# Chunked attention with a mixture of experts on one core: weight loads from iteration 19 on, a reordered prologue, deeper output buffers, and the conditional in front of slot 22

## The chip, the core and the metric

The kernel runs on one core of one Trainium2 chip. The metric is device time in microseconds (us). PE is the matrix engine, PEld its weight loads, DVE, ACT and POOL are the vector, scalar and general engines, SP issues most DMAs. POOL issues DMAs too, those that cast or scatter; they are called software DMAs below, because the profile lists them under `software_dynamic`.

## What is computed

```python
# attention, per batch b and head h, in 24 chunks of 32 queries
k_full = concat([mem_k, k[l_start:r_end]])     # 8 memory rows, then 16 + 32 + 8 rows of context
a = softmax(q_c @ k_full.T / 8)
x[token] = a @ concat([mem_v, v[l_start:r_end]])        # 3072 tokens, 8 heads x 64 = 512
# then a dense part and a mixture of 8 experts, one expert a token
y_dense = relu(x @ w1_dense) @ w2_dense
logits = x @ w_gate;  e = argmax(logits)
y_moe = softmax(logits)[e] * (relu(x @ w1[e]) @ w2[e])
out = y_dense + y_moe
```

## The kernel before, in words

The order of the instructions on every engine is the order of the program: the schedule is written by hand. A tile is 128 tokens, and there are 24 of them.

**Prologue** (lines 522 to 550). POOL issues the loads of k and q, a pair of heads each (`load_qk`). SP issues the memory rows of V (`load_mem_rows`, 8 small DMAs), the first V tile (`load_v(0)`), the gate's weights and `load_v(1)`. DVE clears `kbds[0]` and `mkbd`, the block-diagonal keys of the first batch and of the memory. `transposes(0)` gives eight steps, k and q by turns for four head pairs: PE transposes, ACT copies q; of k ACT copies the half of the first head (L352) and DVE that of the second (L350). After each second step DVE clears a quarter of `kbds[1]` (L545). Then `mem_keys` turns the memory keys.

**Attention loop** (L600). Iteration i holds stages of several tiles: the scores of tile i, turning and values of the tiles before, the gate and the dense part of older ones. On DVE an iteration has one `mx` (L385). `qk_at` gives the k and q loads of an iteration, and at odd i `load_v((i + 5) // 2)` issues ten or more DMAs on SP. `shift(i)` copies V rows within and between V tiles (L294, L297), so it needs the next V tile. In iteration 0 POOL and DVE make constants; in iteration 3 POOL asks for the first half of the dense weights; in iteration 4 come the table constants (L165 to L182). In the iterations of `W_AT`, 16 to 21, `next_w` asks for one half of an expert's weights each. The list starts with both halves of expert 0, the second dense half, then both halves of expert 1, of 2 and so on, 17 in all. Finished rows of x go to the DRAM buffer `xs` with `scatter` (L515), an indirect DMA on POOL, sorted by expert.

**End of the loop** (L652 to L685). The last stages are written out; one `next_w` stands in their middle.

**Slots** (`run`, L854). A slot is 128 rows of one expert. 28 slots always run, and 14 more stand in two nested conditionals (L899, L901) behind them; on these inputs they are not taken. In slot n: `between(n)` may ask for weights (`W_SLOT`), `bring` finds the weights of the next slot, `first` is the first matmul (L802), `second` the dense and the expert's second one (L818, L821), `turn` transposes the rows of the next slot, `send` scales, adds and issues the output (L847, an indirect DMA on POOL). The rows of a slot come with `fetch`, a DMA on SP, six slots ahead. `send` writes `gw`, `to` and `o`, which have three buffers each; `to` and `o` are free again when their output has landed. Slots 0 to 2 are of experts 0, 1 and 2.

The value that decides the conditional (`nov`, computed on DVE in the first slots) is read by every engine with `values_load` at L897, after the last slot.

Of the kernel before, what the change touches and what calls it, by code (L numbers as in the profile page):

```python
# [48 lines left out]
W_AT = (16, 17, 18, 19, 20, 21)  # L49
W_SLOT = (1, 2, 4, 6, 7, 9, 10, 12, 13, 15)  # L50
SOON = 9
NXG = 6
EARLY = 3
# [5 lines left out]
def kernel(  # L59
# [149 lines left out]
    with ExitStack() as one:  # L209
# [152 lines left out]
        def attention(g, qT, kbd):  # L362
# [4 lines left out]
            def scores():  # L367
                sc = ps.tile([128, H, KEYS], F32, tag="ps", name="sc")
                for hp in range(HP):
                    nc.tensor.matmul(sc[:, 2 * hp:2 * hp + 2, CTX:],  # L370
                                     qT[:, hp, 128 * t:128 * t + 128],
                                     mkbd[:, b * HP + hp], start=True, stop=True)
                for hp in range(HP):
                    for cc in range(4):
                        n0 = 128 * t + 32 * cc
                        nc.tensor.matmul(sc[32 * cc:32 * cc + 32, 2 * hp:2 * hp + 2, :CTX],  # L376
                                         qT[:, hp, n0:n0 + 32],
                                         kbd[:, hp, :, n0:n0 + CTX],
                                         start=True, stop=True, tile_position=(0, 32 * cc))
# [5 lines left out]
                nc.vector.reduce_max(mx, sc, axis=AX.X)  # L385
# [145 lines left out]
        for _ in range(2 * (HP - 1)):  # L531
            load_qk()
        load_mem_rows(0, B)
        load_v(0)
        nc.vector.memset(kbds[0], 0.0)  # L535
        nc.vector.memset(mkbd, 0.0)
        load_mk()
        make_identity(nc, identf)
        nc.sync.dma_start(wgate, moe_w_gate.rearrange("(t p) m -> p t m", p=128))
        load_v(1)  # L540
        turned, steps = transposes(0)
        for n, step in enumerate(steps):
            step()
            if n % 2:
                nc.vector.memset(kbds[1][:, n // 2], 0.0)  # L545
        mem_keys()
# [53 lines left out]
        for i in range(NT):  # L600
# [84 lines left out]
        scatter(n)  # L685

# [14 lines left out]
    with ExitStack() as two:  # L701
# [61 lines left out]

        first_x = w2.tile([128, 1], F32, name="first_x", bufs=1)

        def fetch(j):
            xg = w3.tile([128, ROW], F32, tag="xg", name="xg", bufs=NXG)
# [6 lines left out]
        def turn(j):  # L774
# [4 lines left out]
            xT = w3.tile([128, DT + FT, 128], BF16, tag="xT", name="xT", bufs=2)  # L779
# [4 lines left out]
        def bring(j):  # L784
# [7 lines left out]
            wa = w2.tile([128, DT, 512], BF16, tag="wa", name="wa")  # L792
# [40 lines left out]
        def send(j):  # L833
            xg = xgs.pop(j)
            gw = w3.tile([128, 1], F32, tag="gw", name="gw")
            nc.vector.reciprocal(gw, xg[:, ROW - 2:ROW - 1])  # L836
            to = w3.tile([128, 1], I32, tag="to", name="to")
# [6 lines left out]
            o = w3.tile([128, DM], F32, tag="o", name="o")  # L844
# [38 lines left out]
        for j in js[EARLY:EARLY + NXG - 1]:  # L883
            fetch(j)
        def between(n):
# [3 lines left out]
            if n in W_SLOT:  # L889
                next_w()  # L890

# [5 lines left out]
        count = nc.values_load(nov[:1, :1], min_val=0, max_val=NOVER)  # L897

        with tc.If(count > SURE - SLOW, preferred_fallthrough_block=False):  # L899
# [33 lines left out]
```

## Time and profile before

| | |
|---|---|
| median of 3 runs | 268.08 us (266.94 to 270.17) |
| the profiled execution | 266.79 us |
| its span, first to last instruction | 265.1 us |
| PE busy | 214.4 us (81%) |
| DVE, ACT, POOL busy | 167.6, 148.8, 146.9 us |
| mean granted PE clock | 0.947 |
| software DMAs | 28.38 MB, 55.4% of the DMA engines' span |
| DMAs issued by SP | 17.46 MB, 29.0% |
| HBM | 45.26 MB read, 15.76 MB written |

A row of the timeline reads: start, duration, engine, line, operation, out<-in, shapes, count, and in brackets the idle time of the engine before it and what ended it. A q behind an engine's name is its sequencer, which waits, branches and issues. "issue" stands for idle time that nothing in the profile explains. A row of the waits reads: who waited, for whom, us in total, how often, the longest.

### The profile page before, as it was taken

To read this page: it belongs to the slowest core of one execution; us is meant where nothing else is said; L and a number is where in the kernel's file an instruction comes from. 1 tells how busy PE (TensorE), PEld (TensorE's weight loads), DVE (VectorE), ACT (ScalarE), POOL (GpSimd) and SP (SyncE) were. 2 spreads that over 40 slices of the span, in tenths; PEclk is the share of its full clock that TensorE was granted. 3 is DMA by queue.
4 is the path that set the end of the run, shared out by engine and by line. 5 is a ranking of instruction groups with operands and counts; after the bars stand their busy time and mean duration, and the time that the engine had idled before them with its cause. 6 is when DMAs were issued, how large, how long until landed. Compare 5 with 4: busy or idle time off the path is not lost. (4 is left out here: it accounts for less than half of the span.)

```text
span 265.1 us, 9702 instructions
## 1 busy us (share of the span) xinstructions
PE 214.4 (81%) x3808; PEld 161.6 (61%) x3843; DVE 167.6 (63%) x421; ACT 148.8 (56%) x279; POOL 146.9 (55%) x228
## 2 busy tenths in 40 slices
PE   1545889998999985973997797999899998999930
PEld 1324677787787874752785674667566665666710
DVE  7566866889889996844598623884454343556520
ACT  2534766976896776470476463556455555455520
POOL 8748334697777985653376654344545352333420
PEclk9999967999999999796599999999999999999995
DMA  6999975799989999999773195599999999551120
GB/s 87 184 198 180 186 127 100 130 176 222 205 205 193 227 230 161 195 163 233 124 123 122 42 190 223 163 239 294 260 271 203 270 285 259 174 161 53 48 109 2
DMA packets 56833, 46.50 MB, mean 175 GB/s; under 512 B 30158, under 2 KB 49102, under 8 KB 56784
## 3 DMA queue, kind: packets, MB, share of 16 engines
q0 software_dynamic: 22656, 28.38, 55.4%
q1 hardware_dynamic: 34128, 17.46, 29.0%
q8 instruction: 32, 0.52, 0.8%
q14 instruction: 17, 0.14, 0.2%
HBM read 45.26 MB, written 15.76 MB: 230 GB/s over the span
## 5 line engine op out<-in xcount | busy, mean ns | idle before, releaser
L847 POOL DMA_INDIRECT out_dram<-o,to x28 | 31.1, 1109 | 52.1 <-DVE o L845 42.4
L781 ACT COPY xT<-xt 128x512 bf16<-128x512 bf16 x28 | 16.4, 585 | 39.6 <-DVE gw L836 35.5
L845 DVE TENSOR_TENSOR o<-py,oe 128x512 f32<-128x512 f32 x28 | 19.3, 690 | 20.7 <-ACT oe L843 19.2
L515 POOL DMA_INDIRECT xs<-row,si x24 | 26.4, 1099 | 9.3 <-issue 4.0
L440 POOL CAST xT<-x 128x512 bf16<-128x512 f32 x22 | 13.6, 616 | 31.0 <-ACT x L437 28.2
L821 PE MATMUL py<-wall,h 128*128 128x512 bf16 (+1 forms) x111 | 28.7, 379 | 1.0 <-DMA wall<-in_moe_w_dram 1.0
L448 PEld LDWEIGHTS pg<-wgate,x 128*128 128x128 f32 x192 | 26.5, 202 | 4.5 <-ACT x L437 1.0
L409 PE MATMUL xp<-vw,aT 64*32 64x65 f32 x1280 | 20.4, 240 | 9.3 <-DVE vw L297 6.1
L392 ACT ACTIVATE a<-a 128x512 f32<-128x512 f32 x24 | 15.1, 630 | 22.6 <-DVE a L387 21.4
L455 PE MATMUL ph<-wall,xT 128*128 128x512 bf16 x75 | 23.6, 403 | 4.4 <-ACT a L392 1.8
L352 ACT COPY kbd<-tp 64x768 bf16<-64x768 bf16 x28 | 22.1, 790 | 7.9 <-DVE kbd L535 4.2
L818 PE MATMUL py<-wall,xT 128*128 128x512 bf16 x99 | 25.9, 379 | 0.8
L428 POOL CAST row<-xn 128x512 bf16<-128x512 f32 x24 | 21.3, 886 | 8.7 <-DVE xn L421 8.5
L448 PE MATMUL pg<-wgate,x 128*128 128x8 f32 x192 | 24.6, 255 | 0.1
L409 PEld LDWEIGHTS xp<-vw,aT 64*32 64x32 f32 x1280 | 15.9, 113 | 13.9 <-issue 7.1
L294 DVE COPY vw<-vw 24x1820 f32<-24x1820 f32 x17 | 21.1, 1240 | 0.7 <-DMA vw<-in_v_dram 0.2
L385 DVE TENSOR_REDUCE mx<-sc 128x8 f32<-128x512 f32 x24 | 16.6, 690 | 7.1 <-PE sc L376 6.5
L843 ACT ACTIVATE oe<-py,gw 128x512 f32<-128x512 f32 x28 | 19.4, 692 | 2.1 <-PE py L821 2.1
L397 PE MATMUL ap<-identf,a 128*128 128x128 f32 x96 | 17.1, 306 | 4.2 <-ACT a L392 4.0
L802 PEld LDWEIGHTS <-wall 128*128 128x128 bf16 x256 | 15.6, 98 | 5.3 <-issue 2.0
L437 ACT COPY x<-xtp 128x512 f32<-128x512 f32 x24 | 14.1, 586 | 7.5 <-PE xtp L435 6.6
L421 DVE TENSOR_TENSOR xn<-xp,rs 128x512 f32<-128x512 f32 x24 | 16.6, 692 | 2.3
(162 smaller groups left out, 464.8 us busy)
## 6 DMA issues: line engine op xcount, KB each, us to landing
wall<-in_moe_w_dram POOLq DMA_DIRECT2D x16, 512.0 KB, 9.4
xg<-xs SPq DMA_DIRECT2D x25, 257.0 KB
kb<-in_k_dram POOLq DMA_DIRECT2D x16, 192.0 KB, 6.5
qb<-in_q_dram POOLq DMA_DIRECT2D x16, 192.0 KB, 6.7
vw<-in_v_dram SPq DMA_DIRECT2D x48, 64.0 KB
xs<-wall SPq DMA_DIRECT2D x8, 257.0 KB
vw<-in_v_dram SPq DMA_DIRECT2D x32, 56.0 KB
vw<-mtpl SPq DMA_DIRECT2D x20, 65.0 KB
```

Of the source, the lines that this page charges most:

```text
L294: eng(vw[r + 32:r + 56, :PC - 1], vw[r:r + 24, 1:])
L352: nc.scalar.copy(dst, tv[r])
L409: nc.tensor.matmul(xp[32 * cc:32 * cc + 32, par, (D + 1) * hp:(D + 1) * (hp + 1)], st["aT"][r, hp, 32 * cc:32 * cc + 32], vw[r, 4 * (g % 2 ...
L428: nc.gpsimd.tensor_copy(row[:, :XW].bitcast(BF16), st["xn"])
L448: nc.tensor.matmul(grp["pg"][:, u, :], st["x32"][:, d, :], wgate[:, d, :], start=(d == 0), stop=(d == DT - 1))
L455: nc.tensor.matmul(ph, st["xT"][:, d, :], wall[:, E, d, :], start=(d == 0), stop=(d == DT - 1))
L515: i = nc.gpsimd.indirect_dma_start(xs[:, :], bass.IndirectOffsetOnAxis(ap=grp["si"][:, u:u + 1], axis=0), row.bitcast(I32), None, bounds_c ...
L818: nc.tensor.matmul(py, xts[j][:, DT + f, :], wall[:, E, DT + f, :], start=(f == 0), stop=(f == FT - 1))
L821: nc.tensor.matmul(py, hs[j][:, f, :], w[:, f, :], start=(f == 0), stop=(f == FT - 1))
L843: nc.scalar.activation(oe, hs[j, False], AF.Copy, scale=gw)
L845: nc.vector.tensor_tensor(o, hs[j, True], oe, ALU.add)
L847: i = nc.gpsimd.indirect_dma_start(out[:, :], bass.IndirectOffsetOnAxis(ap=to, axis=0), o, None, bounds_check=NT * 128 - 1, oob_is_err=False)
```

## The change

Four parts of the program change.

1. Weights. `W_AT` becomes 19 to 23, five in place of six; a second `next_w` stands behind the last `scatter`. The first half of the dense weights is asked for in iteration 4 in place of 3.
2. Prologue. POOL loads k and q of two head pairs, then the memory keys, then the other two pairs. `load_v(0)`, the gate's weights and `load_v(1)` come after the fourth transposing step, and so does `mem_keys`. `kbds[0]` is cleared in quarters, each in front of its steps; the last quarter of `kbds[1]` is cleared in iteration 0, and the table constants are made there too. The scores' two loops over head pairs become one.
3. Buffers. `gw` and `o` have six buffers, `to` has eight.
4. Conditional. The value is read, and the 14 conditional slots stand, in front of slot 22 in place of behind slot 27. Their `xg`, `xT` and `wa` have tiles of their own (the tag's added "m").

```diff
-W_AT = (16, 17, 18, 19, 20, 21)
+W_AT = (19, 20, 21, 22, 23)
+REST = 22
...
                     nc.tensor.matmul(sc[:, 2 * hp:2 * hp + 2, CTX:], ...
-                for hp in range(HP):
                     for cc in range(4):
...
-        for _ in range(2 * (HP - 1)):
+        for _ in range(2):
             load_qk()
         load_mem_rows(0, B)
-        load_v(0)
-        nc.vector.memset(kbds[0], 0.0)
+        load_mk()
+        for _ in range(4):
+            load_qk()
+        make_identity(nc, identf)
         nc.vector.memset(mkbd, 0.0)
-        load_mk()
-        make_identity(nc, identf)
-        nc.sync.dma_start(wgate, moe_w_gate.rearrange("(t p) m -> p t m", p=128))
-        load_v(1)
         turned, steps = transposes(0)
         for n, step in enumerate(steps):
+            if n % 2 == 0:
+                nc.vector.memset(kbds[0][:, n // 2], 0.0)
             step()
-            if n % 2:
+            if n == 3:
+                mem_keys()
+                load_v(0)
+                nc.sync.dma_start(wgate, moe_w_gate.rearrange("(t p) m -> p t m", p=128))
+                load_v(1)
+            if n % 2 and n < 2 * HP - 1:
                 nc.vector.memset(kbds[1][:, n // 2], 0.0)
-        mem_keys()
...
             if i == 0:
+                nc.vector.memset(kbds[1][:, HP - 1], 0.0)
                 constants()
-            if i == 3:
+                table_constants()
+            if i == 4:
                 load_w(E, 0)
-            if i == 4:
-                table_constants()
...
         scatter(n)
+        next_w()
...
-            gw = w3.tile([128, 1], F32, tag="gw", name="gw")
+            gw = w3.tile([128, 1], F32, tag="gw", name="gw", bufs=6)
...
-            to = w3.tile([128, 1], I32, tag="to", name="to")
+            to = w3.tile([128, 1], I32, tag="to", name="to", bufs=8)
...
-            o = w3.tile([128, DM], F32, tag="o", name="o")
+            o = w3.tile([128, DM], F32, tag="o", name="o", bufs=6)
...
+        def rest():
+            own[0] = "m"
+            with tc.If(count[0] > SURE - SLOW, preferred_fallthrough_block=False):
+                start(more[:2])
+                with tc.If(count[0] > SURE - SLOW + 2, preferred_fallthrough_block=False):
+                    start(more[2:])
+            own[0] = ""
...
             if n in W_SLOT:
                 next_w()
+            if n == REST:
+                count.append(nc.values_load(nov[:1, :1], min_val=0, max_val=NOVER))
+                rest()
...
-        count = nc.values_load(nov[:1, :1], min_val=0, max_val=NOVER)
-        with tc.If(count > SURE - SLOW, preferred_fallthrough_block=False):
-            start(more[:2])
-            with tc.If(count > SURE - SLOW + 2, preferred_fallthrough_block=False):
-                start(more[2:])
```

More of the change, by code (lines that the diff above doesn't have):

```diff
@@ L762, in table @@
                                         op0=ALU.is_gt, op1=ALU.mult)]
+        own = [""]
         first_x = w2.tile([128, 1], F32, name="first_x", bufs=1)
         def fetch(j):
-            xg = w3.tile([128, ROW], F32, tag="xg", name="xg", bufs=NXG)
+            xg = w3.tile([128, ROW], F32, tag="xg" + own[0], name="xg", bufs=NXG)
             read_rows(xg, rowi[:, j:j + 1])
@@ L791, in bring @@
             ev = nc.vector.value_load(expi[:1, k:k + 1], min_val=0, max_val=n - 1)
-            wa = w2.tile([128, DT, 512], BF16, tag="wa", name="wa")
+            wa = w2.tile([128, DT, 512], BF16, tag="wa" + own[0], name="wa")
             nc.vector.tensor_copy(
@@ L884 @@
             fetch(j)
+        def rest():
[5 more added lines that the diff above has]
+            own[0] = ""
+        count = []
         def between(n):
```

2 lines of the change are left out of this document (1 added, 1 removed).

## The prediction

> **What bounds the kernel now.** I read the page first (span, clock and DMA slices), then the windows around the throttled stretches, then the timeline of the stages that the edits touch.
>
> ```profile
> span 265.1 us, 9702 instructions
> DMA  6999975799989999999773195599999999551120
> 107.40:110.90 3.50, 3.28 (x56) 2.23 (x50) 3.05 (x5) 1.97 (x4) 2.96 (x3) 0.51 1.10 219
> 121.10:131.30 10.20, 7.46 (x130) 5.89 (x132) 5.41 (x10) 2.09 (x4) 2.01 (x3) 0.50 0.96 184
> 163.40:253.20 89.80, 85.40 (x870) 58.53 (x884) 48.21 (x148) 48.20 (x83) 38.67 (x39) 1.00 0.81 206
> ```
> In the window rows the columns are stretch, length, busy time of PE, PEld, DVE, ACT and POOL, granted clock, DMA share, GB/s. From 163.4 on (the expert slots) PE is busy 85.4 of 89.8 us: a stall of PE there is lost time. Before that the DMA engines are full (9s) up to about 125 us, and twice the clock is halved.
>
> ```profile
> 94.65 0.68 DVE L385 TENSOR_REDUCE mx<-sc 128x8 f32<-128x512 f32 x1
> 97.14 0.85 POOL L91 DMA_DIRECT2D wall<-in_moe_w_dram  x1
> 106.08 0.38 PE L376 MATMUL sc<-kbd,qT 128*32 128x112 bf16 x16 [2.88 <-issue]
> 110.02 6.25 SPq L275 DMA_DIRECT2D vw<-in_v_dram  x8
> 122.98 0.29 DVE L297 COPY vw<-vw 24x260 f32<-24x260 f32 x1 [2.61 <-DMA vw<-in_v_dram]
> 123.62 1.40 PE L409 MATMUL xp<-vw,aT 64*32 64x65 f32 x58 [6.12 <-DVE vw L297]
> 135.27 0.68 DVE L385 TENSOR_REDUCE mx<-sc 128x8 f32<-128x512 f32 x1
> 139.33 0.69 DVE L385 TENSOR_REDUCE mx<-sc 128x8 f32<-128x512 f32 x1
> 145.17 0.69 DVE L385 TENSOR_REDUCE mx<-sc 128x8 f32<-128x512 f32 x1
> ```
> L385 starts once an iteration; these rows are iterations 15, 21, 22 and 23. The first weight goes out at 97.14, in iteration 16. SP issues the V loads one behind the other, eight in 6.25 us from 110.02. PE stands 2.88 us with no releaser shown and 6.12 us for V rows of iteration 19, and each stall brings a halved clock.
>
> **The change part by part** (minus is time gained).
>
> Weights from iteration 19 on. Iterations 16 to 23 take 145.17 - 94.65 = 50.5 us. Undisturbed, I put iteration 16 at 4.3 us, 17 at 5.0 (transposes), 18 to 20 at 4.3, 21 at 4.9 (it chooses experts), 22 at 4.06 (139.33 - 135.27), and 23 at 5.84 as it was (145.17 - 139.33): 37.0. The 4.3 and 4.9 are estimates just above the 4.06 row. Three weights leave the stretch in which the last V loads run, so these land before iterations 18 to 21 ask for them. But five weights now run beside iterations 19 to 23, so I add 1.6 us, half of such a stall as 2.88 us: 38.6, a gain of **-11.9**. Ends: -13.5 with no stall; -4.3 with two stalls of 2.88, each with a halved 3.4 us window (1.7 us).
>
> The dense weights one iteration later (3 to 4):
> ```profile
> 33.31 0.71 POOL L236 DMA_DIRECT2D qb<-in_q_dram  x1
> 41.64 0.61 PE L455 MATMUL ph<-wall,xT 128*128 128x512 bf16 x1
> DMA to landing us min/median/max: 8.2/9.9/10.7
> ```
> The issue would follow the q load of 33.31, some 7.6 us ahead of its first use at 41.64, against 8.2 to 10.7 us of landing: up to 3 us of wait. Against it, the early V loads have the DMA engines to themselves for one iteration longer. I take **0**, ends -3 and +3.
>
> The prologue:
> ```profile
> 6.50 0.79 ACT L352 COPY kbd<-tp 64x768 bf16<-64x768 bf16 x1 [4.17 <-DVE kbd L535]
> 7.33 0.96 DVE L350 COPY kbd<-tp 64x768 bf16<-64x768 bf16 x1 [0.78 <-ACT kbd L352]
> 8.52 0.72 DVE L545 MEMSET kbd<- 128x792 uint32 x1 [0.23 <-issue]
> 2.71 0.27 DVE L266 MEMSET ve<- 32x256 f32 x1
> 15.46 0.85 PE L339 MATMUL tp<-ident,qb 128*64 128x128 bf16 x12 [0.47 <-DMA qb<-in_q_dram]
> 15.87 0.96 DVE L350 COPY kbd<-tp 64x768 bf16<-64x768 bf16 x1 [0.96 <-ACT kbd L352]
> 17.77 0.46 DVE L327 COPY mkbd<-mkt 64x128 bf16<-64x128 bf16 x2
> 18.32 0.17 DVE L142 MEMSET ones<- 128x128 bf16 x1
> 19.42 0.69 DVE L385 TENSOR_REDUCE mx<-sc 128x8 f32<-128x512 f32 x1
> 35.40 0.17 DVE L173 CAST thr<-thr_i 128x22 f32<-128x22 int32 x1
> 36.82 0.15 DVE L182 MEMSET low<- 128x1 f32 x8
> ```
> Before, PE waits for k and q from DMA (0.47 us at the last one). V(0) and its loads on SP now stand behind the fourth transpose, so k and q land earlier, though the two memory-key loads pass four of them on POOL's queue. But the clearing of kbds[0], one memset before, becomes four, each on DVE in front of its pair of copies, and DVE's copy waits for ACT's (7.33 follows 6.50 + 0.79). So for each head pair now follow one another: clear 0.72, ACT copy 0.79, DVE copy 0.96, gap 0.23, clear of kbds[1] 0.72, some 0.13 between them: 3.55 us, more than DMA needs. From the first DVE copy at 6.96 (ACT no longer waits the 0.4 us for the long memset) three such rounds, the copy 0.96 and what step 3 puts in between (L327 0.46, four memsets of 0.27, gaps 0.1) end the last copy at 20.2, against 15.87 + 0.96 = 16.8. Behind it on DVE, ahead of the first mx, stand 0.23 + 0.72 for the last clear, 0.17 for ones, POOL's select and first iota (an estimate: 0.6 with the hand-overs), the table constants (35.40 to 36.97, 1.6 us), and 0.3: mx at 23.9 instead of 19.42, **+4.5**. All PE work waits for it. What leaves iteration 4 was beside PE work there: 0 back. V(0), wgate and V(1) queue on SP behind memsets that end at about 13; V(0) is first read in iteration 1, so this hides. Ends: -2.4 (the copies hide and k and q set the pace, 15.46 becoming 13), +6.
>
> Experts' slots:
> ```profile
> 163.94 0.97 POOL L515 DMA_INDIRECT xs<-row,si  x1 [0.30 <-issue]
> 171.71 1.03 PE L821 MATMUL py<-wall,h 128*128 128x512 bf16 x4
> 188.24 1.05 PE L802 MATMUL ph<-xT,wa 128*128 128x128 bf16 x16
> 192.69 1.05 PE L802 MATMUL ph<-xT,wa 128*128 128x128 bf16 x16 [1.23 <-DVE xT L780]
> DVE to L839 <- DMA out_dram<-o,to: 12.2, 11, 2.9
> 224.87 1.02 PE L821 MATMUL py<-wall,h 128*128 128x512 bf16 x4 [0.95 <-DMA wall<-in_moe_w_dram]
> ```
> The last weight of expert 2 now goes out after the last scatter (163.94 + 0.97 = 164.9) and slot 2 wants it at 171.71, 6.8 us later, with landings of 8.2 to 10.7 measured in a fuller DMA: **+1.2**, ends 0 and +3.2. It also stands on POOL ahead of the first reads' marker and runs beside these reads.
>
> Deeper buffers: DVE waits 12.2 us for old output rows before it can write `to`; of this PE feels what a slot lasts beyond its PE work, 85.40 / 28 = 3.05 us by the window row: 1.4 us at the quoted slot (192.69 - 188.24 = 4.45). For the other ten waits together I estimate 1.2 us, since most are shorter than DVE's slack: -2.6. Faster slots meet the same weights, and the wait of 0.95 at 224.87 grows by about 1: **-1.6**, ends -3.1 and +0.5.
>
> The conditional in front of slot 22, and the end:
> ```profile
> L899 PEldq COMPARE_BRANCH  x2: 93/2070/4047, 254.0 to 254.6; - x2
> L899 ACTq COMPARE_BRANCH  x2: 38/44/49, 254.8 to 255.1; - x2
> L899 POOLq INC_SWDGE_SEM  x1: 1147/1147/1147, 258.9 to 258.9; - x1
> L928 POOLq DRAIN  x3: 51/103/3992, 260.3 to 264.8; - x3
> 253.21 1.02 PE L821 MATMUL py<-wall,h 128*128 x4
> 255.96 0.97 POOL L847 DMA_INDIRECT out_dram<-o,to  x1 [1.46 <-DVEq L899]
> ```
> PE's second branch, over the slots not taken, lasts 4.05 us, from 254.6 to 258.65, 4.4 us after the last matmul (253.21 + 1.02). At the end this hides behind POOL; in front of slot 22 six slots of PE work queue behind it. With its restart 4.7 us. Such a stop halves the clock: stops of 2.88 and 6.12 us left halved stretches of 3.4 and 10.2 us, the latter with 7.7 us after PE had resumed at 123.62; between them I take 5.2 us at half speed, 2.6 us. Together **+7.3**. ACT's branches take 0.05 us and DVE's work has slack. On POOL all output rows must land and 1.15 us follows, with slot 22's output behind it; PE's own stop covers that. Ends: +1.0 (branch as short as ACT's, the loads remain), +8.6.
>
> [...]
>
> At the end the last output starts at 255.96 and the span ends 9.1 us later: landing at about 258.9 (INC_SWDGE_SEM waits for it), 1.15, POOL's 3.99 us drain, 0.8. Without the conditional the drain can start once the output is issued: 1.0 + 4.0 + 0.8 = 5.8, **-3.3**. Ends -1.2 (only INC_SWDGE_SEM goes) and -4.6 (the drain shrinks). The merged loop of the scores only orders 20 matmuls anew: 0; the extra tags take SBUF alone: 0.
>
> Sum: -11.9 + 0 + 4.5 + 1.2 - 1.6 + 7.3 - 3.3 = -3.8. The profiled execution took 266.79, so 263.0; the median of the runs is 1.29 above it, so 264.3.
>
> **The rivals.** (a) The prologue gets faster: DVE's copies need not follow ACT's, and k and q set the pace. Against it stand four waits on ACT in the rows of that kind. Term -2.0 instead of +4.5: 257.8. (b) PE's branch costs what ACT's does, the target being loaded already: term +1.0: 258.0. Against it: 4.05 us over the same untaken slots. [...] (c) The slower side: weights at 19 to 23 stall PE twice as at 106.08, since DMA is still full of V loads there. Term -4.3: 271.9. All other terms add to +8.1, so the kernel is slower from the point at which this gain falls under 8.1. For it speaks that the DMA slices read 9 to about 125 us; against it that the last V loads move earlier.
>
> **How the numbers follow.** The sum 0.46 (own range 260 to 268.5), (a) 0.15, (b) 0.15, (c) 0.20, others 0.04. The range 257.5 to 272 reaches from the two fast rivals to the slow one. A measurement tells about 1% from no change: 265.4 and 270.8 are the bounds. Of the sum's 0.46 some 0.27 lies below 265.4 and 0.17 within; with (a) and (b) at 0.13 each and part of others, faster 0.54, same 0.25, slower 0.21.
>
> **What would show it.** The first mx near 24 us (wrong if under 20); no wait for V rows in iterations 18 to 20, and mx of iterations 15 to 23 some 38 to 39 us apart; a PE pause over 4 us with a halved clock ahead of slot 22; no `to` waits for output rows; POOL's drain starting within 2 us of the last output. A short branch, or two stalls beside the moved weights, would make the prediction wrong.

## The result: 6.6% slower

The changed kernel takes 286.19 us (median of four runs, 285.34 to 289.64), the kernel before, run beside it, 268.53 us (266.94 to 270.17). The ratio is 1.066 with a 95% interval of 1.058 to 1.073: some 17.6 us more, where 3.8 us less were forecast. The comparisons leave disturbed executions out (where too few are left for an interval, medians of all runs are given), and since the profiled execution of the changed kernel (289.64 us) is a disturbed one, the same kernel was profiled once more (`after_again`, 278.33 us).

From the page of the changed kernel:

```profile
span 287.9 us, 9730 instructions
...
PEclk9999997589999999997999857979999999795998
DMA  6996959479999998558999572999999999250111
```

A digit stands for 7.2 us here. The DMA engines are full (9s) to about 108 us only, where before they were to about 125; a new full stretch, from about 137 to 158 us, goes with the moved weights (issued from 130.80 to 152.08 us), and the clock is halved in more places. The stages, as windows that end at the mx of iterations 0, 7, 15 and 23, at the first matmul of slots 0, 4, 21, 24 and 27, and at the end (columns: stretch, length, busy time of PE, PEld, DVE, ACT and POOL, clock, DMA share, GB/s). Before:

```profile
0.00:19.42 19.42, 7.79 (x117) 5.50 (x117) 12.22 (x29) 7.75 (x10) 13.21 (x42) 1.00 1.06 155
19.42:54.68 35.26, 29.22 (x675) 24.21 (x679) 26.68 (x61) 23.72 (x42) 19.66 (x38) 0.90 0.97 142
54.68:94.65 39.97, 38.21 (x1030) 31.55 (x1036) 35.44 (x69) 30.96 (x67) 33.15 (x53) 1.00 1.07 210
94.65:145.17 50.52, 38.21 (x828) 30.80 (x835) 34.66 (x77) 28.99 (x53) 30.30 (x44) 0.86 0.88 170
145.17:163.38 18.21, 14.53 (x291) 10.72 (x291) 9.46 (x38) 8.48 (x26) 9.96 (x15) 1.00 0.55 142
163.38:175.84 12.46, 12.32 (x127) 8.49 (x129) 8.84 (x36) 6.44 (x11) 6.09 (x8) 1.00 0.69 179
175.84:232.18 56.34, 52.62 (x535) 36.09 (x544) 27.20 (x82) 29.79 (x51) 24.68 (x26) 1.00 1.04 253
232.18:242.00 9.82, 9.38 (x95) 6.35 (x96) 5.70 (x17) 5.14 (x9) 3.39 (x3) 1.00 0.38 123
251.32:265.09 13.77, 2.92 (x25) 1.56 (x23) 1.69 (x6) 2.40 (x4) 2.40 (x3) 0.73 0.15 54
```

The changed kernel:

```profile
0.00:23.80 23.80, 8.57 (x117) 5.94 (x117) 13.36 (x47) 7.54 (x10) 14.08 (x50) 1.00 0.92 134
23.80:67.95 44.15, 35.33 (x673) 27.67 (x677) 25.57 (x46) 24.14 (x42) 20.02 (x32) 0.85 0.80 126
67.95:111.37 43.42, 42.43 (x1006) 33.93 (x1016) 34.25 (x69) 31.24 (x66) 34.17 (x51) 1.00 1.01 196
111.37:153.53 42.16, 40.18 (x866) 31.07 (x866) 34.38 (x76) 28.88 (x53) 29.12 (x43) 0.96 0.79 156
153.53:178.62 25.09, 20.42 (x291) 14.91 (x292) 10.14 (x38) 8.92 (x26) 10.88 (x18) 0.73 0.62 141
178.62:195.17 16.55, 13.98 (x126) 9.44 (x128) 9.31 (x37) 6.72 (x12) 6.34 (x8) 0.90 0.87 186
195.17:252.35 57.18, 53.98 (x536) 37.13 (x544) 26.82 (x80) 29.94 (x52) 24.32 (x25) 0.97 0.99 237
252.35:268.45 16.10, 11.88 (x97) 7.91 (x97) 5.82 (x15) 5.52 (x10) 3.56 (x4) 0.79 0.26 79
277.65:287.94 10.29, 2.92 (x25) 1.57 (x23) 1.61 (x5) 2.41 (x4) 2.31 (x3) 0.89 0.18 67
```

| stage | before | changed | changed, second trace | change forecast |
|---|---|---|---|---|
| to the first mx | 19.42 | 23.80 | 23.79 | +4.5 |
| mx of iterations 0 to 7 | 35.26 | 44.15 | 40.02 | 0 |
| 7 to 15 | 39.97 | 43.42 | 44.78 | 0 |
| 15 to 23 | 50.52 | 42.16 | 43.76 | -11.9 |
| 23 to slot 0 | 18.21 | 25.09 | 19.78 | 0 |
| slots 0 to 3 | 12.46 | 16.55 | 13.78 | +1.2 |
| slots 4 to 20 | 56.34 | 57.18 | 55.09 | -1.6 |
| slots 21 to 23 | 9.82 | 16.10 | 16.13 | +7.3 |
| slots 24 to 26 | 9.32 | 9.20 | 9.20 | 0 |
| slot 27 to the end | 13.77 | 10.29 | 10.29 | -3.3 |
| span | 265.09 | 287.94 | 276.62 | -3.8 |

The first mx, slots 21 to 23 and the tail moved as forecast. Three stages forecast at 0 grew. From the changed kernel's timeline, the waits of PE that answer to this (rows as in the front part):

```profile
48.92 0.58 PE L455 MATMUL ph<-wall,xT 128*128 128x512 bf16 x1 [4.48 <-DMA wall<-in_moe_w_dense_dram]
161.70 0.27 PE L409 MATMUL xp<-vw,aT 64*32 64x65 f32 x2 [2.08 <-issue]
189.13 0.62 PE L784 MATMUL xt<-ident,xg 128*128 128x128 bf16 x8 [2.46 <-DMA xg<-xs]
259.58 1.86 PE L808 MATMUL ph<-xT,wa 128*128 128x128 bf16 x16 [4.00 <-issue]
```

The dense weights are late in iteration 5; something that the profile doesn't name holds PE up behind the loop; the first rows are late in front of slot 3; the branch stands in front of slot 22. Windows over the stretches behind the first two:

```profile
46.80:60.40 13.60, 10.92 (x134) 8.26 (x136) 3.52 (x7) 5.10 (x8) 2.95 (x4) 0.50 0.71 118
162.80:176.50 13.70, 13.26 (x62) 9.44 (x62) 4.16 (x22) 5.33 (x14) 4.96 (x8) 0.50 0.61 155
```

With waits of 4.48 and 2.08 us the clock goes to a half for 13.7 us each. Behind the end of the first wait 11.5 us of this are left, so 5.7 us are lost to the clock; behind the second all of it, 6.8 us: more than the waits themselves cost. And in stage 7 to 15, where nothing waits long, seven of the eight iterations are longer.

The theory going into the experiments: the four mechanisms of the forecast hold, and two edits put at 0 cost the rest (the merged loop of the scores, the dense weights one iteration later), with the weights themselves disturbing what follows the loop. The rivals: the slow iterations come from the loads that were moved; the halved clocks are chance; the gain of the moved weights isn't what it looks like.

### The profile page after: what moved, and what is told of

It is laid out like the page before. It is cut to its first block, busy times and chain, and to the rows that moved or that the text cites. A ratio compares the mean times of both kernels' runs of the same rounds, so it can differ in the third digit from the quotient of the medians.

```text
span 287.9 us, 9730 instructions
## 1 busy us (share of the span) xinstructions
PE 238.8 (83%) x3808; PEld 175.9 (61%) x3843; DVE 166.9 (58%) x424; ACT 150.5 (52%) x279; POOL 148.7 (52%) x228
## 5 line engine op out<-in xcount | busy, mean ns | idle before, releaser
L515 POOL DMA_INDIRECT xs<-row,si x24 | 28.8, 1202 | 14.6 <-issue 6.5
L440 POOL CAST xT<-x 128x512 bf16<-128x512 f32 x22 | 13.6, 619 | 38.9 <-ACT x L437 36.4
L455 PE MATMUL ph<-wall,xT 128*128 128x512 bf16 x75 | 27.2, 458 | 7.2 <-DMA wall<-in_moe_w_dense_dram 4.5
L448 PEld LDWEIGHTS pg<-wgate,x 128*128 128x128 f32 x192 | 29.0, 218 | 4.7 <-issue 1.1
L824 PE MATMUL py<-wall,xT 128*128 128x512 bf16 x99 | 28.3, 404 | 0.9 <-issue 0.2
L448 PE MATMUL pg<-wgate,x 128*128 128x8 f32 x192 | 26.6, 265 | 0.0
L385 DVE TENSOR_REDUCE mx<-sc 128x8 f32<-128x512 f32 x24 | 16.6, 691 | 14.1 <-PE sc L376 13.7
L376 PE MATMUL sc<-kbd,qT 128*32 128x112 bf16 x384 | 23.2, 232 | 0.1
L397 PE MATMUL ap<-identf,a 128*128 128x128 f32 x96 | 17.1, 307 | 7.1 <-ACT a L392 6.6
L786 DVE COPY xT<-xt 128x512 bf16<-128x512 bf16 x28 | 11.8, 423 | 18.2 <-PE xt L784 15.6
L811 ACT ACTIVATE h<-ph 128x512 bf16<-128x512 f32 x28 | 16.7, 597 | 9.5 <-PE ph L808 7.4
L428 POOL CAST row<-xn 128x512 bf16<-128x512 f32 x24 | 18.6, 775 | 5.6 <-DVE xn L421 5.5
L457 ACT ACTIVATE row<-ph 128x512 bf16<-128x512 f32 x24 | 14.3, 598 | 13.3 <-PE ph L455 12.4
```

The lines of the kernel that those rows point to most:

```text
L428: nc.gpsimd.tensor_copy(row[:, :XW].bitcast(BF16), st["xn"])
L448: nc.tensor.matmul(grp["pg"][:, u, :], st["x32"][:, d, :], wgate[:, d, :], start=(d == 0), stop=(d == DT - 1))
L455: nc.tensor.matmul(ph, st["xT"][:, d, :], wall[:, E, d, :], start=(d == 0), stop=(d == DT - 1))
L515: i = nc.gpsimd.indirect_dma_start(xs[:, :], bass.IndirectOffsetOnAxis(ap=grp["si"][:, u:u + 1], axis=0), row.bitcast(I32), None, bounds_c ...
L824: nc.tensor.matmul(py, xts[j][:, DT + f, :], wall[:, E, DT + f, :], start=(f == 0), stop=(f == FT - 1))
```

## The experiments

Ratios are to the kernel before, run beside them on the same chip, with 95% intervals; 1% is 2.7 us. Where the time of a single slot is given, it is that from the first matmul of the slot ahead to its own.

**The changed kernel again** (`after_again`, no edit).

> The changed kernel unchanged, as a control for the runs beside it. Expected 285 to 287 us and every loss at the place where the first profile has it: iteration 5 near 12 us, iterations 7 to 15 near 48.5 us, from the mx of iteration 23 to slot 0 near 25 us (18.2 before). If the last loss was of that one execution alone (its halved clock from 162.8 to 176.5 us), this profile shows about 19 to 22 us there and a span some 3 to 4 us shorter.

Measured: 1.066 (1.054 to 1.077). The later first mx, the longer iterations 8 to 15 and the branch are there again, and two losses in other sizes (the table): behind the loop 1.6 us in place of 6.9, slots 0 to 3 1.3 in place of 4.1. The loss at the dense weights is not there:

```profile
41.30 1.88 PE L448 MATMUL pg<-wgate,x 128*128 128x8 f32 x8
49.58 1.02 PE L455 MATMUL ph<-wall,xT 128*128 128x512 bf16 x4 [0.63 <-DMA wall<-in_moe_w_dense_dram]
50.44 0.95 PE L448 MATMUL pg<-wgate,x 128*128 128x8 f32 x8
```

PE waits 0.63 us for them, with no halved stretch behind it, and the profiled execution (278.33 us) is the fastest of the changed kernel; its other times are 284.34 to 289.64 us. That iterations 0 to 7 still take 40.02 us has another reason: the row at 41.30 lasts twice as long as the same work at 50.44, so PE runs at half speed there. The trace has no record of the clock before 48.8 us (36.5 in the first trace), and where there is none the clock column reads 1.00. So these losses vary from one execution to the next; they are no fixed price.

**The merged loop** (`before_merged`, and over pairs `before_pairs`, on the kernel before).

```diff
-                for hp in range(HP):
                     for cc in range(4):
```

```diff
+                for h0 in range(0, HP, 2):
+                    for hp in range(h0, h0 + 2):
                         nc.tensor.matmul(sc[:, 2 * hp:2 * hp + 2, CTX:], ...
+                    for hp in range(h0, h0 + 2):
                         for cc in range(4):
```

> The kernel before with the two loops of the scores made one, nothing else. Theory (each change between a matmul over the whole array and the four on a quarter of its columns costs PE about 0.05 us, seven more pairs of them an iteration): the scores of a tile take 1.1 us instead of 0.67, 24 times, so +8 to +11 us, 276 to 279 us. Rival (the slow iterations 7 to 15 of the changed kernel come from loads that were moved, and the order of the scores is free, as I predicted): 267 to 269 us.

> The kernel before with the loops of the scores made one over pairs: two matmuls over the whole array, then their eight on quarters, twice. By the theory of a price for each change of shape there are 3 changes inside a tile in place of 7 (merged) and 1 (before), so a third of what the merged loop costs: +2.5 to +4 us, 271 to 273 us. If instead one fixed delay at the start of the scores is the cause, it would be all or nothing: near the merged kernel or near the kernel before.

Measured: 1.0105 (1.0015 to 1.0196) merged, 1.007 (0.984 to 1.030) in pairs. PE's rows of one tile's scores, up to the next work. Before:

```profile
58.44 0.25 PE L370 MATMUL sc<-mkbd,qT 128*128 128x16 bf16 x4
58.62 0.38 PE L376 MATMUL sc<-kbd,qT 128*32 128x112 bf16 x16
58.93 0.66 PE L435 MATMUL xtp<-identf,xn 128*128 128x128 f32 x4
```

In pairs:

```profile
62.02 0.20 PE L371 MATMUL sc<-mkbd,qT 128*128 128x16 bf16 x2
62.15 0.28 PE L377 MATMUL sc<-kbd,qT 128*32 128x112 bf16 x8
...
62.71 0.66 PE L436 MATMUL xtp<-identf,xn 128*128 128x128 f32 x4
```

Merged (the changed kernel):

```profile
71.89 0.17 PE L371 MATMUL sc<-mkbd,qT 128*128 128x16 bf16 x1
72.00 0.23 PE L376 MATMUL sc<-kbd,qT 128*32 128x112 bf16 x4
72.16 0.18 PE L371 MATMUL sc<-mkbd,qT 128*128 128x16 bf16 x1
...
73.00 0.65 PE L435 MATMUL xtp<-identf,xn 128*128 128x128 f32 x4
```

From the first matmul of the scores to the next work: 0.49, 0.69 and 1.11 us with 1, 3 and 7 changes between the full shape and the quarter shape. That is 0.10 us a change, both times. The price on PE is as the theory says, 0.62 us a tile, 15 us over 24; but the time grew by 2.8 us only. In the trace of `before_merged` the mx of iteration 15 comes at 105.06, 10.4 us later than before, that of 23 at 147.92, only 2.7 later: the waits for V rows in iterations 17 to 20 are gone. They had hidden the price. Not all of the 10.4 us is the loop's: in this trace PE is at half speed up to 48.3 us (eight gate matmuls take 1.88 us at 40.33, 0.95 at 48.95), in the one of before up to 28.9 and again from 35.8 to 42.6. (Each tile changes shape, so the price that shows depends on the slack behind it.)

**The dense weights** (`after_dense3` on the changed kernel, `before_dense4` on the kernel before).

```diff
-            if i == 4:
+            if i == 3:
                 load_w(E, 0)
```

This is the edit of `after_dense3`; `before_dense4` takes the step of the change, from 3 to 4.

> The changed kernel with the first half of the dense weights asked for in iteration 3 again. Theory (the 4.48 us wait for them and the halved clock behind it, 46.8 to 60.4 us, cost iterations 5 and 6 together 8.5 us): 8 to 9 us faster than the changed kernel, 277 to 279 us, with no wait for the dense weights. Rival (the clock would have been halved there anyhow, as it was from 35.8 to 42.6 us before): only 3 to 5 us faster, 281 to 283 us.

> The kernel before with the first half of the dense weights asked for in iteration 4 in place of 3, nothing else. In the changed kernel this step was worth 8.8 us (285.86 against 277.05). Theory (issued about 33 to 34 us, wanted at 41.6, landing late beside q, k and V loads: PE waits and the clock halves): a wait of 2 to 4.5 us at the first dense matmul and 5 to 9 us more at mx of iteration 7; part of it comes back at the waits for V rows, so 2 to 8 us slower than before. Rival (only the later prologue made the weights late): no wait for them and within 2 us of before.

Measured: the changed kernel gets from 285.86 to 277.05 us (medians of four runs each), its ratio from 1.066 to 1.0305 (1.019 to 1.042). The kernel before with the weights in iteration 4 gets to 1.006 (0.998 to 1.013). The wait is there (POOL's issue, then PE):

```profile
34.12 0.77 POOL L91 DMA_DIRECT2D wall<-in_moe_w_dense_dram  x1
42.74 0.58 PE L455 MATMUL ph<-wall,xT 128*128 128x512 bf16 x1 [2.07 <-DMA wall<-in_moe_w_dense_dram]
```

Around it the clock is halved from 38.1 to 51.7 us (a wait of 1.75 us for V rows stands ahead of it), and mx of iteration 15 is at 103.76, 9.1 us late: 4.7 us of it are there at mx of iteration 7, most of the rest comes in iteration 10, with a pause of 1.67 us put down to "issue" and a halved clock from 72.2 to 79.0 us. But the mx of iteration 23 is at 144.38, 0.8 us early. So one step costs 8.8 us in one kernel and about 1.5 in the other (-0.5 to 3.5 by its interval), and in these traces the difference lies behind iteration 15, in what was waiting there.

**The moved weights alone** (`before_weights`, and the same kernel again, `before_weights2`).

```diff
-W_AT = (16, 17, 18, 19, 20, 21)
+W_AT = (19, 20, 21, 22, 23)
...
         scatter(n)
+        next_w()
```

> The kernel before with the weights alone moved (iterations 19 to 23 and one behind the last scatter), the dense weights still in iteration 3. Theory (the weights stood in the way of the last V loads): the waits for V rows go, mx of iterations 15 to 23 shrinks from 50.5 to 38 to 40 us, and slots 3 and 4 give back 2 to 4 us for the last weight of expert 2: 7 to 10 us faster than before. Rival (the V loads were late by themselves, and PE now waits for the five weights): within 3 us of before.

> The kernel before with the weights alone moved (iterations 19 to 23 and one behind the last scatter), a second time. If the move takes the weights out of the way of the last V loads whatever happens ahead of them: again 0.97 to 0.99 of before, no wait for V rows, mx of iterations 15 to 23 38 to 40 us. If it depends on how far PE is ahead of the V loads by then (the weights go out at PE's pace, the V loads at the DMA engines' pace): a profile in which iteration 15 comes early (mx near 94 us) has waits of 4 to 8 us for V rows again, the mx of iteration 23 is near 145 us whatever iteration 15 did, and the time is within 1.5% of before.

Measured: 0.980 (0.969 to 0.991) at first, 0.999 (0.993 to 1.004) the second time; the medians of all runs are 271.92 us beside 271.95, and 268.12 beside 269.27. In both traces iteration 15 comes late by chance (mx at 98.70 and 98.91) and no V wait follows. The kernel with deeper buffers beside it (`before_weights_buf`) is the same program up to the slots; there iteration 15 came early, and the wait is back:

```profile
94.44 0.68 DVE L385 TENSOR_REDUCE mx<-sc 128x8 f32<-128x512 f32 x1
...
117.51 0.29 DVE L297 COPY vw<-vw 24x260 f32<-24x260 f32 x1 [4.28 <-DMA vw<-in_v_dram]
```

In `before_weights2`:

```profile
98.91 0.68 DVE L385 TENSOR_REDUCE mx<-sc 128x8 f32<-128x512 f32 x1
...
117.20 1.04 DVE L297 COPY vw<-vw 24x260 f32<-24x260 f32 x2
```

The second copy of iteration 18's V rows ends its wait at 117.51 in the one; in the other the row at 117.20 holds both copies, and neither waits. The first theory holds in part: in the eight traces with weights from iteration 16 or 18 on in which this copy waits, it starts at 119.4 to 129.3 us, and with the weights from 19 on and a wait at 115.3 to 117.5, so the weights in their way do make the V rows later. What falls is that the wait goes whatever happens ahead: a PE that is 4 us later waits nowhere, an early one still waits. That mx of iteration 23 stays near 145 us didn't come out either: it is at 136.86, 139.86 and, with the wait, 142.14.

**Where the weight of expert 2 goes** (`before_w18` without the last `next_w`, `before_w19` with two of them in iteration 23).

```diff
-W_AT = (16, 17, 18, 19, 20, 21)
+W_AT = (18, 19, 20, 21, 22, 23)
```

```diff
-W_AT = (16, 17, 18, 19, 20, 21)
+W_AT = (19, 20, 21, 22, 23, 23)
...
-            if i in W_AT:
+            for _ in range(W_AT.count(i)):
                 next_w()
```

> The kernel before with the weights asked for in iterations 18 to 23 and none behind the last scatter, nothing else. Against the same with 19 to 23 and one behind the last scatter (0.98 of before): if the last weight of expert 2 causes the wait for the first rows in front of slot 3, slots 3 and 4 take 3.1 us each again and the kernel is 2 us faster than that one, 0.965 to 0.975 of before; mx of iterations 15 to 23 38 to 40 us. Rival (the wait in front of slot 3 comes from the scattered rows themselves, or the weight in iteration 18 meets the V loads): 0.98 to 1.0 of before.

> The kernel before with weights in iterations 19 to 23, two of them in 23, and none behind the last scatter. Theory (the weight behind the last scatter runs beside the first reads of rows): slots 3 and 4 take 3.1 to 3.3 us, mx of iterations 15 to 23 stays at 38 to 40 us, and the kernel is as fast as the one with the weight behind the scatter or up to 2 us faster: 0.965 to 0.98 of before. Rival (the rows come late by themselves): slot 3 still over 4.5 us.

Measured: `before_w18` 270.60 us beside 273.47 for before (medians, no interval): unclear. `before_w19` 1.023 (1.007 to 1.040): slower by the interval, though by how much isn't clear. In both, slots 3 and 4 take 3.1 to 3.3 us each, and with the weight behind the last scatter slot 3 takes 4.9 to 5.1 in all three traces (two of `before_weights`, one of `before_weights_buf`), with this row of `before_weights2`:

```profile
171.11 0.62 PE L779 MATMUL xt<-ident,xg 128*128 128x128 bf16 x8 [1.73 <-DMA xg<-xs]
```

So that wait is the last weight's, 1.9 us. (Only `after_dense3`, with the weight in the same place but its first slots at half clock up to 177.3 us, has 3.07 us for slot 3.) But the other places cost as much. With iteration 18, PE waited 4.35 us for V rows. With two weights in 23:

```profile
153.53 0.31 PE L409 MATMUL xp<-vw,aT 64*32 64x65 f32 x1 [3.05 <-issue]
```

behind which the clock is halved from 152.6 to 169.7 us, and from the mx of iteration 23 to slot 0 it takes 26.7 us (26.7 again in `before_w19_buf`). In iteration 21 PE also waited 7.7 us for DVE, which waited 7.05 for V rows, with mx of iteration 15 at 93.70: an early PE again.

**What "issue" is** (`before_shift`: 64 small matmuls more in the prologue, whose result is not used).

```diff
             step()
+            if n == 1:
+                dm = ps.tile([128, 128], F32, tag="ps", name="dm")
+                for _ in range(64):
+                    nc.tensor.matmul(dm[:32, :1], ident[:, :32], ident[:, :1],
+                                     start=True, stop=True)
```

> The kernel before with 64 small matmuls more between the second and the third transposing step, where PE waits for loads anyway; their result is not used. In the traces so far PE's longer pauses with no releaser (0.9 to 3.5 us) stand in front of the records 705, 2241, 5057 and 5825 of PE's instructions (4033 in the first trace of before), which differ by multiples of 256. Theory (PE's instructions are fetched in blocks of 256, and a block comes late where the DMA engines are full): the pauses keep these record numbers, so in the code they move 128 records forward: the one at the values of the third tile (L409 before) falls into the scores ahead of them (L376). Rival (the pauses belong to a hand-over at that place of the program): they stay at the values (L409) and their record numbers grow by 128. The time should stay within 3 us of before by both.

Measured: 270.26 us (one run). Its pauses:

```profile
38.76 0.23 PE L376 MATMUL sc<-kbd,qT 128*32 128x112 bf16 x3 [0.97 <-issue]
...
64.99 1.02 PE L409 MATMUL xp<-vw,aT 64*32 64x65 f32 x50 [1.40 <-issue]
...
95.00 0.71 PE L409 MATMUL xp<-vw,aT 64*32 64x65 f32 x34 [1.53 <-issue]
...
113.59 0.42 PE L409 MATMUL xp<-vkeep,aT 64*32 64x65 f32 x21 [2.57 <-issue]
...
119.44 0.33 PE L409 MATMUL xp<-vw,aT 64*32 64x65 f32 x11 [1.02 <-issue]
```

Counted through PE's and PEld's records these are 961, 2236, 3511, 4276 and 4531. 705 plus multiples of 256 gives 961, 2241, 3521, 4289 and 4545; the trace lacks 35 of 7974 records, so later numbers fall up to 14 short. All five fit, 256 or a multiple of it apart. The one at 2241 stood at a transpose (L339) in other traces and stands at the values now: it kept its number and moved in the code. So these pauses go with the count of PE's instructions and not with a place in the program; that PE waits there for its own instructions, in blocks of 256, is argued from this. The DMA trace fits it: the queue q8, of the kind `instruction`, moves packets of 16 KB, 33 here, and each of the five pauses ends 1.2 to 1.8 us after one has landed; so do 60 of all 61 pauses of PE over 0.9 us that the 20 traces put down to "issue", those at the branch in front of slot 22 among them. That a block comes late because of other DMA traffic is argued, not shown. (No pause fell on 705 itself this time, the place I had named.)

Two of these numbers, 705 plus 17 and 20 times 256, are 5057 (iteration 22) and 5825 (the last values behind the loop, where PE pauses 2.08 us in the changed kernel). What lies behind the loop is long where the clock is halved there: from the mx of iteration 23 to slot 0 it takes 18.2 us at a mean clock of 1.00 (before), 18.4 at 1.00 (`after_d3_prologue`), 22.4 at 0.77 (`before_weights`), 25.1 at 0.73 (changed), 26.7 at 0.68 (`before_w19`). In the nine traces with weights from iteration 16 or 18 on (before, and `before_` merged, pairs, buffers, dense4, cond, shift, w18, w18_buf) it takes 17.0 to 18.9 us; in the eleven with weights from 19 on 18.4 to 26.7, 23.0 on average. That the later weights cause this is argued from these two groups; `before_w18` has loads in 19 to 23 as well, and against `before_weights` each of its loads comes only one place earlier.

**The rest of the changed kernel undone, one part each, beside the dense weights** (`after_d3_loops`, `after_d3_end`, `after_d3_prologue`; compared with `after_dense3`, 1.0305).

```diff
+                for hp in range(HP):
                     for cc in range(4):
```

```diff
-            if n == REST:
-                count.append(nc.values_load(nov[:1, :1], min_val=0, max_val=NOVER))
-                rest()
...
             [n + NXG] * (EARLY <= n < len(js) - NXG))
+        count.append(nc.values_load(nov[:1, :1], min_val=0, max_val=NOVER))
+        rest()
```

The third has the prologue, the clearing and the constants of the kernel before (the removed lines of the diff in the front part, from the loads of k and q to `table_constants`).

> The changed kernel with the dense weights in iteration 3 and the two loops of the scores apart again. An iteration in which nothing waits took 0.62 us more with the merged loop (5.11 for 4.50, iteration 7), yet the kernel before lost only 2.7 us by it up to the mx of iteration 23, for its waits for V rows shrank by 7.6 us. Theory (in the changed kernel those waits are gone, and so is what hid the price): 7 to 11 us faster than the same kernel with the merged loop (277.05), 266 to 270 us. Rival (a faster PE runs into the V loads again): 2 to 3 us faster, 274 to 275 us, with waits for V rows in iterations 16 to 20.

> The changed kernel with the dense weights in iteration 3 and the conditional behind slot 27 again. Theory (PE's branch over the slots not taken costs 6 to 7 us with its halved clock in front of slot 22 and hides at the end, where POOL's drain costs 3.5 us more): 2.5 to 4 us faster than the same kernel with the conditional in front of slot 22 (277.05), 273 to 274.5 us; slots 22 and 23 take 3.1 to 3.7 us each, the tail 13.7 us. Rival (slots 22 and 23 are slow for another reason): slot 22 stays over 6 us and only the tail moves, 280 us.

> The changed kernel with the dense weights in iteration 3 and the prologue, the clearing and the constants as before. Theory (all of PE's work starts 4.4 us earlier, and nothing behind it waits for DMA): first mx at 19.4 us and the end 4 to 5 us earlier than with the new prologue (277.05), 272 to 273 us. Rival (the loads set the pace of the attention loop, so an earlier start only lengthens waits): first mx at 19.4, but mx of iteration 23 less than 2 us earlier, 275 to 277 us.

Measured: the two loops 1.010 (1.000 to 1.021), so 5.5 us faster than with the merged loop, between theory and rival: an iteration is 0.6 us shorter where nothing waits (4.51 for 5.11 us in iteration 7), but PE then pauses 2.84 us at record 2241 and runs at half clock from 72.1 to 79.0 us, so that iteration 10 takes 9.3 us and mx of iteration 23 is only 1.6 us earlier. The conditional at the end 1.010 (0.985 to 1.034): the interval is too wide for a verdict; the trace shows where time is won and lost. Slot 22 with the conditional in front (`after_dense3`):

```profile
249.22 1.86 PE L808 MATMUL ph<-xT,wa 128*128 128x128 bf16 x16 [4.16 <-issue]
```

and with it at the end:

```profile
245.99 1.05 PE L808 MATMUL ph<-xT,wa 128*128 128x128 bf16 x16 [0.35 <-DVE xT L786]
```

Slots 22 and 23 take 6.7 us in place of 12.0, the tail 13.4 in place of 10.3: 2.2 us net. The old prologue 1.029 (1.018 to 1.041): no change that can be told, though the first mx is at 20.47, 3.6 us earlier. It was lost again in iteration 4, where PE paused 3.52 us at record 705 and ran at half clock from 38.9 to 49.1 us; mx of iteration 7 was 3.4 us later than with the new prologue. The rival came out here, though by a pause and not by loads.

**The conditional alone** (`before_cond`: part 4 of the change on the kernel before).

> The kernel before with the conditional in front of slot 22, nothing else. Theory (PE's branch of 4 us, the restart at half clock, less POOL's drain at the end): slots 22 and 23 together 12.5 to 13.5 us in place of 6.7, the tail 10.3 in place of 13.8 us: 2.5 to 4 us slower, 1.01 to 1.015 of before. Rival (it cost this only where the weights were late): slots 22 and 23 under 9 us, and the kernel not slower.

Measured: 1.020 (1.007 to 1.034). Slots 22 and 23 take 13.6 us in place of 6.7, the tail 10.45 in place of 13.8: +3.5 us, inside the interval.

**The deeper buffers** (`before_buffers`, `before_w18_buf`, `before_w19_buf`, `before_weights_buf`; each is compared with its kernel without them).

```diff
-            gw = w3.tile([128, 1], F32, tag="gw", name="gw")
+            gw = w3.tile([128, 1], F32, tag="gw", name="gw", bufs=6)
...
-            to = w3.tile([128, 1], I32, tag="to", name="to")
+            to = w3.tile([128, 1], I32, tag="to", name="to", bufs=8)
...
-            o = w3.tile([128, DM], F32, tag="o", name="o")
+            o = w3.tile([128, DM], F32, tag="o", name="o", bufs=6)
```

> The kernel before with the deeper gw, to and o alone. Prediction's step: DVE's 12.2 us of waits for old output rows go, slots 9, 11 and 15 lose their excess of 1.4, 0.4 and 0.8 us, and 1 us comes back at the last weight of expert 7: -1.6 us. Rival (the excess only moves to the next late weight): slots 4 to 21 together take as long as before, 59.6 us, and the time is the same within 0.5 us.

> The kernel before with the weights in iterations 18 to 23 and the deeper output buffers: the two parts of the change that should help, without the others. If their gains add (5 to 8 us and 1.6 us), 0.96 to 0.975 of before, faster than both kernels. If the later weights and the faster slots meet at the last weight of expert 7, the buffers bring nothing here: the same as the kernel with the weights alone.

> The same with the deeper output buffers as well. If the buffers help, slots 4 to 21 take 1 to 2 us less than without them; if the excess only moves to the next late weight, the same within 0.5 us. Against before 0.96 to 0.98.

> The same with the deeper gw, to and o. If the buffers help by themselves: 1 to 2 us less than the kernel beside it, and slots 4 to 21 take 1 to 2 us less. If their excess only moves to late weights: the same within 0.5 us. If both parts help, 0.965 to 0.985 of before and the fastest kernel of the study.

Measured: medians without and with the buffers 273.47 and 270.80, 270.60 and 273.69, 274.18 and 272.75, 268.12 and 267.70 us; to before only the last has an interval, 1.004 (0.980 to 1.028). The times tell nothing. The traces tell more, from the start of slot 4 to that of slot 21: 56.34 without and 55.17 with buffers, 59.06 and 57.35, 57.02 and 55.81, 57.48 and 54.59: 1.2 to 2.9 us less each time. These are single executions, and all those without the buffers range over 54.9 to 59.1 us, so the size is uncertain. What is shown is that DVE's waits for old output rows are gone, which read in `before_weights2`

```profile
DVE to L840 <- DMA out_dram<-o,to: 13.8, 9, 3.4
```

No kernel of the study beats the kernel before beyond doubt. The moved weights with the buffers, the two parts that looked like gains, end at 1.004.

## Why the prediction was wrong

**Held, step by step.** The prologue: first mx at 23.80, forecast 23.9, and by the mechanism named: ACT and DVE in turn behind the clears (in the changed kernel DVE clears for 0.72 us from 8.77, ACT copies for 0.79 from 9.57, DVE for 0.96 from 10.40). The conditional: slots 21 to 23 grew by 6.3 us in both traces, forecast 7.3; the tail shrank by 3.5, forecast 3.3. The deeper buffers: 1.2 to 2.9 us in four pairs of single traces, forecast 1.6. The waits for V rows in iterations 18 to 20 are gone, and mx of iterations 15 to 23 shrank by 8.4 and 6.8 us with the merged loop's 8 times 0.62 = 5.0 us in it: the forecast 11.9 stands there to the eye.

**Failed: "The merged loop of the scores only orders 20 matmuls anew: 0".** It costs 0.10 us at each of six more changes of shape, 0.62 us a tile on PE; undone in the changed kernel it gives back 5.5 us (from two ratios that are each uncertain by 1%; by the medians of all runs, each beside its kernel before, only 1 us). The rows of before showed the two shapes only in blocks, so this term should have had a bound and had none.

**Failed: the dense weights "0, ends -3 and +3".** 8.8 us in the changed kernel; the intervals of the two ratios, 1.054 to 1.077 and 1.019 to 1.042, don't meet. The landing was read rightly (8.8 us from the issue on). POOL's rows in the first trace:

```profile
39.37 0.73 POOL L237 DMA_DIRECT2D qb<-in_q_dram  x1
40.10 1.32 POOL L92 DMA_DIRECT2D wall<-in_moe_w_dense_dram  x1
```

What I left out is that the q load ahead of the issue would itself come 6 us later in the changed kernel, while PE wanted the weights only 2.8 us later (44.44 for 41.64; before, a pause of 1.77 us and a halved clock stand ahead of that matmul): 4.3 us were left in place of the 7.6 forecast. And behind the wait of 4.48 us the clock stayed halved for 11.5 us: half of that, 5.7 us, is more than the wait. It isn't in every execution: where PE came late by itself (second trace), the wait was 0.63 us.

**Failed most: the sum itself, with "-11.9" as a gain beside delays.** The wait for V rows is slack: the V loads go at the pace of the DMA engines (busy at a share of 1.07 in stage 7 to 15 of before, 0.88 in 15 to 23), and what holds PE up ahead of iteration 16 shortens that wait. Two kernels that keep the weights in 16 to 21 show it: with iteration 15 late at 105.06 (`before_merged`) or 103.76 (`before_dense4`), mx of iterations 15 to 23 takes 42.9 and 40.6 us, much like the changed kernel's 42.2. In that one iteration 15 comes at 111.37, so the wait would have been gone without moving a weight. That it gained nothing there is argued from those two kernels; it wasn't run in the changed one, and a late iteration 15 isn't always enough (100.31 in `before_shift`, where DVE still waits 6.28 us for V rows in iteration 21 and the stage takes 49.4 us). The same 8 to 12 us were booked as a gain, when they were already the cover that made other delays cheap. Alone, with no other edit ahead, the move gave 0.980 at first and 0.999 in the repeat. In its traces mx of iteration 23 does come early, at 136.9, 139.9 and 142.1 us, against 144.4 to 152.1 in the seven with weights in 16 to 21; but slot 4 starts at 173.6, 175.5 and 176.4, and before at 175.8. What the loop gains is lost again behind it.

**Mis-sized: what the moved weights disturb.** "23 to slot 0" was 0 in the sum, and the last weight of expert 2 1.2 us. Measured +6.9 and +1.6 behind the loop, +4.1 and +1.3 in slots 0 to 3: the first rows come late beside the last weight (shown: 1.9 us), and behind the loop the clock is halved after pauses of PE at record 5825 (2.08 us, then 13.7 us at half clock, in the changed kernel). With the weights alone moved it is +1.9 to +4.2 behind the loop and +1.7 to +1.9 in slots 0 to 3. That the weights make these pauses longer is argued, not shown. (A slip beside it: the 1.6 us added for a stall in iterations 19 to 23 is called half of 2.88, which is 1.4.)

Undoing gives the account: 8.8 us for the dense weights, 5.5 for the merged loop, 2.2 to 5.6 for the conditional, nothing that can be told for the prologue. That is 16.5 to 19.9 of the 17.6 us; what is left, the moved weights with the buffers, would be near zero, as `before_weights_buf` (1.004) has it. As each term is a difference of ratios that are uncertain by 1% or more, the agreement supports the account and doesn't prove it. Rival (c) gave the right sign, but for another reason: in iterations 19 to 23 no pause of PE over 0.9 us is in the first trace of the changed kernel and one, of 1.41 us at record 5057, in the second. What stays open is why pauses of the same length leave 3.4 us of half clock in one execution and 10 to 17 in another, and the share of chance in the repeat of the moved weights.

## What to carry to other kernels

Before a wait is counted as a gain, ask what sets its end: if that is the pace of the DMA engines, the wait is slack, it hides delays ahead of it (in `before_merged` 10.4 us at iteration 15 were 2.7 us at iteration 23), and its removal and those delays don't add. Keep matmuls of one shape together, and price a reordering on PE by its changes of shape (0.10 us each here). Ahead of a load that is moved, look for the queue it stands in and for the clock that is lost behind its wait (5.7 us behind 4.48 here), and not at the wait alone.

## What the hardware showed beside this

- A change between a 128-column and a 32-column matmul cost PE 0.10 us: 0.49, 0.69 and 1.11 us for the same 20 matmuls with 1, 3 and 7 changes. What in the change costs (the shape, the place in the array, the place of the output) isn't separated.
- In `before_shift` PE's five pauses with no releaser stand at records 705 plus multiples of 256. At such a record PE lost nothing (705 there) or up to 4.2 us (4289 in `before_cond`), and 60 of the 61 pauses over 0.9 us in the 20 traces end 1.2 to 1.8 us after a 16 KB packet of the queue of the kind `instruction` has landed.
- The halved stretches in these traces last 3.4 us or a multiple of it (3.4, 6.8, 10.2, 13.7, 17.1, 20.5 us). Most go with pauses of PE of 1 to 11 us: up to 252 us, 56 of 68 such stretches in the 20 traces have one over 0.9 us in the 7 us before their start. But stretches of 3.4 us came with no pause over 0.6 us in the 10 us before them as well (132.1 to 135.5 us in the changed kernel).
- PE is at half speed at first, and the clock column doesn't show it: four matmuls of L397 take 1.12 us at 25.50 and 0.66 at 29.47 (before), 1.12 at 35.38 and 0.63 at 40.63 (changed). The first record of the clock comes at 28.5 to 37.3 us in 18 traces and at 48.3 and 48.8 in two; ahead of it the column reads 1.00.
